# A window-attention gradient on one core: computing the gradient of x as (dS·x)·Aᵀ, with dS·x turned by DMA

## The chip, the cores and the metric

The kernel runs on one core of a Trainium2 chip. The metric is the device time of one execution in microseconds; lower is better.

Names used in the profile: PE is TensorE's matmul, PEld its weight load, ACT ScalarE, DVE VectorE, POOL GpSimd, SP SyncE. SPq and POOLq are the queues on which SyncE and GpSimd issue DMAs; the page calls their rings q1 and q0. L126 is line 126 of that run's kernel, so the same operation has other line numbers before and after.

## The reference

Attention in windows of 8x8 pixels on an image of 256x256 pixels with 384 channels, forward and backward:

```python
xw  = windows(x)                       # 1024 windows, 64 tokens, C = 384
q, k, v = split(xw @ wqkv)
p   = softmax(q k^T * C**-0.5)
out = unwindow((p v) @ wo)
# returned: out, and the gradients of x, wqkv, wo for a given grad_out
```

All in bfloat16. The kernel folds the weights once: A = scale·Wq·Wkᵀ, so that the scores are x·A·xᵀ, and B = Wv·Wo, so that the output is P·(x·B). With dS the gradient of the scores, the gradient of x is the sum of three terms: a term of dS with x·Aᵀ (called v in the kernel before), the term of dSᵀ with x·A, and the term of Pᵀ with grad_out·Bᵀ. The last two are called y and z; they are made with channels on the partitions and have to be turned to tokens-on-partitions (`tok`) by a DMA.

## The kernel before

Work goes in quads of four tiles of 128 tokens (two windows each); 128 quads in all. In one step quad c is finished, quad b is in the middle and quad a begins. Everything that SyncE issues goes through one queue, in order:

```python
def load(st):                               # x on SyncE's queue, grad_out on GpSimd's
    ...
    for t in range(QUAD):
        nc.sync.dma_start(out=xq[:, t, :], in_=dram_tile(x, bp, t0 + t))
        nc.gpsimd.dma_start(out=dq[:, t, :], in_=dram_tile(grad_out, bp, t0 + t))

def load_turn(st):                          # dT and xT: both turned by DMA
    ...
            nc.sync.dma_start_transpose(out=dst[:, k:]..., in_=src[:, k:]...)

def to_tokens(st):                          # tok: y and z turned by DMA
    nc.sync.dma_start_transpose(out=tok[:]..., in_=st["yz"][:]...)

def uv(st, t, part):                        # u = x B (part 0) and v = x A^T (part 1)
    wgt, dst, cp = ((B_sb, st["uq"], ...), (AT_sb, st["vq"], ...))[part]
    pj = ring.tile([P, C], F32, tag="r")    # ring: 8 PSUM banks for everything
    for m in range(CK):
        product(pj[:], st["xT"][:, t, m, :], wgt[:, m, :], m == 0, m == CK - 1)
    cp(out=dst[:, t, :], in_=pj[:])

def attend(st, pair, after=None):
    for t in pair:                          # two tiles: 2 x 4 = 8 banks
        po, pu, pw, pd = [ring.tile([P, C], F32, tag="r", name=n) for n in ("po", "pu", "pw", "pd")]
        both((pu, "ST", "xq", True), (po, "PT", "uq", True))     # 64x64 products, four at once
        ...                                 # evictions of po (ACT) and pu (DVE)
        both((pw, "Pb", "dq", True), (pd, "ST", "vq", False))    # pd: the v term of dx
        ...
    for t, pd in made:                      # the y and z terms on top, from tok
        for w, o in ((0, HI), (1, LO)):
            nc.tensor.matmul(pd[o, :], lhsT=st["ps"][:, w, t, :], rhs=st["tok"][:, :, t, w, :], start=False, stop=True)
        ...                                 # eviction (ACT) and store of dx
```

`filler(1)` puts one piece of the weight gradients (24 products, then an addition into `GF_acc` by VectorE, which frees that piece's PSUM bank) before each of the two calls of `attend`.

Of the kernel before, what the change touches and what calls it, by code (L numbers as in the profile page):

```python
# [14 lines left out]
P = 128  # L15
# [7 lines left out]
def kernel(  # L23
# [12 lines left out]









# [7 lines left out]
    scale = float(C) ** -0.5  # L52

    const = ctx.enter_context(tc.tile_pool(name="const", bufs=1))
    setup = ctx.enter_context(tc.tile_pool(name="setup", bufs=1))
    grp = ctx.enter_context(tc.tile_pool(name="grp", bufs=2 * GQ + 1))
    qp = ctx.enter_context(tc.tile_pool(name="qp", bufs=2))
    sm = ctx.enter_context(tc.tile_pool(name="sm", bufs=2))
# [8 lines left out]
    wo_sb = const.tile([P, CK, C], BF16)  # L67
    nc.scalar.dma_start(out=wo_sb[:], in_=wo.rearrange("(m p) n -> p m n", p=P))

    wT_sb = setup.tile([P, JK, C], BF16, tag="big")  # L70
    for jm in range(JK):
        pt = ring.tile([P, C], BF16, tag="r")
        for m in range(CK):
            nc.tensor.transpose(pt[:, m * P:(m + 1) * P], w_sb[:, m, jm * P:(jm + 1) * P], ident[:])
        nc.vector.tensor_copy(out=wT_sb[:, jm, :], in_=pt[:])
# [11 lines left out]
    for dst, left, lo, right, ro, sc in (  # L87
        (A_sb, wT_sb, 0, wT_sb, CK, scale),
        (BT_sb, wo_sb, 0, wT_sb, 2 * CK, None),
        (B_sb, wT_sb, 2 * CK, wo_sb, 0, None),  # L90
        (AT_sb, wT_sb, CK, wT_sb, 0, scale),
    ):
        for mr in range(CK):
            pc = ring.tile([P, C], F32, tag="r")
            for mc in range(CK):
                nc.tensor.matmul(pc[:], lhsT=left[:, lo + mc, mr * P:(mr + 1) * P], rhs=right[:, ro + mc, :],
                                 start=(mc == 0), stop=(mc == CK - 1))
            if sc is None:
                nc.vector.tensor_copy(out=dst[:, mr, :], in_=pc[:])
            else:  # L100
                nc.scalar.activation(out=dst[:, mr, :], in_=pc[:], func=ACT.Copy, scale=sc)
# [8 lines left out]
    OTHER = {0: HI, WT: LO}  # L110
# [9 lines left out]
    def load_turn(st):  # L120
        xq, dq = st["xq"], st["dq"]
        st["xT"] = xT = qp.tile([P, QUAD, CK, P], BF16, tag="xT", name="xT", bufs=3)
        st["dT"] = dT = qp.tile([P, QUAD, CK, P], BF16, tag="dT", name="dT")
        for src, dst in ((dq, dT), (xq, xT)):
            k = G_ON_PE if src is dq else 0
            if k < QUAD:  # L126
                nc.sync.dma_start_transpose(out=dst[:, k:].rearrange("p t m k -> p (t m) k"),
                                            in_=src[:, k:].rearrange("p t c -> p (t c)"))

    def grad_turn(st, t):  # L130
        if t >= G_ON_PE:
            return
        pt = ring.tile([P, CK, P], BF16, tag="r")
        for m in range(CK):
            nc.tensor.transpose(pt[:, m, :], st["dq"][:, t, m * P:(m + 1) * P], ident[:])
        nc.vector.tensor_copy(out=st["dT"][:, t, :, :], in_=pt[:])

    ALL = False
    split = [ALL]

# [7 lines left out]
    ENG = {"D": nc.vector.tensor_copy, "A": nc.scalar.copy}  # L148

    def project(st, kind, mo):  # L150
        if kind == 0 and mo == 0:
            st["yz"] = qp.tile([P, CK, QUAD, 4, WT], BF16, tag="yz", name="yz")
        yz = st["yz"]
        wgt, src = ((BT_sb, st["dT"]), (A_sb, st["xT"]))[kind]
        pj = ring.tile([P, QUAD, 2, WT], F32, tag="r")
# [3 lines left out]
        if kind == 0:  # L159
            ENG[EV["z"][mo]](out=yz[:, mo, :, 0:4:3, :], in_=pj[:])  # L160
        else:
            ENG[EV["y"][mo]](out=yz[:, mo, :, 1:3, :], in_=pj[:])  # L162

# [5 lines left out]
    def scores(st):  # L169
        yz, xT = st["yz"], st["xT"]  # L170
        st["sd"] = sd = ring.tile([P, QUAD, 2, WT], F32, tag="r", name="sd")
        for t in range(QUAD):
            for w in range(2):
                for m in range(CK):
                    product(sd[:, t, w, :], yz[:, m, t, 2 * w:2 * w + 2, :].rearrange("p s k -> p (s k)"),
                            xT[:, t, m, w * WT:(w + 1) * WT], m == 0, m == CK - 1)
# [4 lines left out]
    def soft(st, step):  # L181
# [14 lines left out]
        elif step == 3:  # L196
            ex = st["ex"]
            rs = sm.tile([P, QUAD], F32, tag="rs")
            nc.vector.tensor_reduce(out=rs[:], in_=ex[:], axis=AX.X, op=ALU.add)
            ri = sm.tile([P, QUAD], F32, tag="ri")  # L200
# [3 lines left out]
            st["ps"] = ps = qp.tile([P, 2, QUAD, WT], BF16, tag="ps", name="ps")  # L204
            for w, h in ((0, LO), (1, HI)):
                nc.scalar.copy(out=ps[h, w, :, :], in_=Pb[h, :, :])  # L206
# [6 lines left out]
        else:  # L213
            pd = sm.tile([P, QUAD, WT], F32, tag="pd")
# [4 lines left out]

    def uv(st, t, part):  # L220
        if t == 0 and part == 0:
            for n in ("uq", "vq"):
                st[n] = qp.tile([P, QUAD, C], BF16, tag=n, name=n)
        wgt, dst, cp = ((B_sb, st["uq"], ENG[EV["u"][t]]), (AT_sb, st["vq"], ENG[EV["v"][t]]))[part]
        pj = ring.tile([P, C], F32, tag="r")
        for m in range(CK):
            product(pj[:], st["xT"][:, t, m, :], wgt[:, m, :], m == 0, m == CK - 1)
        cp(out=dst[:, t, :], in_=pj[:])  # L228

    def turn(st):  # L230
        pt = ring.tile([P, QUAD, 2, WT], F32, tag="r", name="pt")
        for t in range(QUAD):
            for w, h in ((0, LO), (1, HI)):
                nc.tensor.matmul(pt[h, t, :, :].rearrange("p s k -> p (s k)"), lhsT=st["ps"][:, w, t, :],  # L234
                                 rhs=ident[:], start=True, stop=True)
        st["PS"] = dst = qp.tile([P, QUAD, 2, WT], BF16, tag="PS", name="PS")
        nc.vector.tensor_copy(out=dst[:], in_=pt[:])

    def turned(st, n, t, h):
        if n in ("PT", "ST"):  # L240
            return st["PS"][h, t, int((n == "ST") == (h == LO)), :]
        return st[n][h, t, :]

    def store(dst, src, bp, t):
        for h, w in ((LO, 1), (HI, 0)):
            nc.gpsimd.dma_start(out=dram_tile(dst, bp, t)[WIN * w:WIN * (w + 1)], in_=src[h, :])  # L246

    def attend(st, pair, after=None):
        bp, t0 = st["at"]
        if pair[0] == 0:  # L250
            st["Uq"] = grp.tile([P, QUAD, C], BF16, tag="Uq", name="Uq")
            st["Wq"] = grp.tile([P, QUAD, C], BF16, tag="Wq", name="Wq")
        def both(straight, crossed):
            for h, o, (dst, lhs, rhs, done) in ((LO, LO, straight), (LO, HI, crossed), (HI, LO, crossed),
                                                (HI, HI, straight)):
                nc.tensor.matmul(dst[o, :], lhsT=turned(st, lhs, t, h), rhs=st[rhs][h, t, :], start=True, stop=done)  # L256

        made = []
        for t in pair:
            po, pu, pw, pd = [ring.tile([P, C], F32, tag="r", name=n) for n in ("po", "pu", "pw", "pd")]  # L260
            both((pu, "ST", "xq", True), (po, "PT", "uq", True))
            osb = ob.tile([P, C], BF16, tag="o")
            ENG[EV["o"][t]](out=osb[:], in_=po[:])  # L263
            ENG[EV["U"][t]](out=st["Uq"][:, t, :], in_=pu[:])  # L264
            both((pw, "Pb", "dq", True), (pd, "ST", "vq", False))
            ENG[EV["W"][t]](out=st["Wq"][:, t, :], in_=pw[:])  # L266
            made.append((t, pd))
            store(out_0, osb, bp, t0 + t)
        for t, pd in made:
            for w, o in ((0, HI), (1, LO)):  # L270
                nc.tensor.matmul(pd[o, :], lhsT=st["ps"][:, w, t, :], rhs=st["tok"][:, :, t, w, :], start=False,  # L271
                                 stop=True)
            dsb = ob.tile([P, C], BF16, tag="d")
            ENG[EV["d"][t]](out=dsb[:], in_=pd[:])  # L274
            store(out_1, dsb, bp, t0 + t)
        if after is not None:
            turn(after)
# [3 lines left out]
    def gf_group(sts):  # L281
        n = len(sts) * QUAD
        for f in range(2):
            for ma in range(CK):
                pw = ring.tile([P, C], F32, tag="r", name="pg")
                for i in range(n):
                    st, t = sts[i // QUAD], i % QUAD
                    product(pw[:], st["xq"][:, t, ma * P:(ma + 1) * P], st["UW"[f] + "q"][:, t, :], i == 0, i == n - 1)
# [11 lines left out]
    def step(c, b, a):  # L300


        def on(st):
            return (lambda f, *r: f(st, *r)) if st is not None else (lambda f, *r: None)
        C_, B, A = on(c), on(b), on(a)
        B(scores)
        B(soft, 0)
        B(uv, 0, 0)
        B(uv, 0, 1)
        B(soft, 1)  # L310
        B(uv, 1, 0)
        B(uv, 1, 1)
        B(soft, 2)
        B(soft, 3)
        B(uv, 2, 0)
        B(uv, 2, 1)
        for t in range(QUAD):
            A(grad_turn, t)
        B(uv, 3, 0)
        B(uv, 3, 1)  # L320
        B(soft, 4)
        for mo in range(CK):
            A(project, 0, mo)
        B(soft, 5)
        filler(1)
        if c is not None:
            attend(c, (2, 3), b)
        else:
            B(turn)
        split[0] = True  # L330
        for mo in range(CK):
            A(project, 1, mo)
        A(to_tokens)
        filler(1)
        split[0] = ALL
        B(attend, (0, 1))

    G_ON_PE = 0
    EV = {"z": "AAA", "y": "AAA", "u": "AAAA", "v": "AAAA", "o": "AAAA", "U": "DDDD", "W": "DDDD", "d": "AAAA"}
    quads = [(bp, t0) for bp in range(NBP) for t0 in range(0, NT, QUAD)]  # L340
    sts = [{"at": q, "i": i} for i, q in enumerate(quads)]
    n = len(sts)
    AHEAD = 3
    with tc.manual_schedule(engines=MANUAL):
        for i in range(min(AHEAD, n)):
            load(sts[i])
            if i < AHEAD - 1:
                load_turn(sts[i])
        held = []
        get = lambda i: sts[i] if 0 <= i < n else None  # L350
        for i in range(-1, n + 1):
            if AHEAD <= i + AHEAD < n:
                load(sts[i + AHEAD])
# [71 lines left out]
```

## Time and profile before

| | before |
|---|---|
| time, median | 2045.04 us of 3 runs (2043.45 to 2060.44) |
| PE, ACT, DVE, POOL busy | 99, 72, 67, 69% |
| SyncE's queue q1, GpSimd's queue q0 | 75.0%, 31.7% of 16 engines' span |
| one step (pu to pu) | 15.62 us |

From the page of the kernel before: the busy time of each engine, the row of DMA busy tenths in 40 slices, the two queues (packets, MB, share of 16 engines' span), and the shares of the chain that ended last.

```profile
PE 2025.2 (99%) x20442; PEld 1148.8 (56%) x20442; DVE 1382.3 (67%) x3107; ACT 1467.0 (72%) x3213; POOL 1419.1 (69%) x2566
...
DMA  9999999999999999999999999999999999999992
...
q1 hardware_dynamic: 873648, 253.80, 75.0%
q0 software_dynamic: 122880, 151.68, 31.7%
...
PE 91%; DMA 2%; ACT 1%; DVE 1%; issue 0%; POOL 0%; ACTq 0%; POOLq 0%
```

PE is busy for nearly the whole span and makes up 91% of the chain, so the kernel is bound by PE. The shares of the two queues add up to 106.7%.

Now the timeline of PE over one pair of `attend` (start in us, length in us, engine, line, operation, number of instructions merged):

```profile
1005.26 0.35 PE L256 MATMUL pu<-xq,PS 64*64 64x384 bf16 x1
...
1005.45 0.33 PE L256 MATMUL pd<-vq,PS 64*64 64x384 bf16 x2
...
1005.77 0.32 PE L256 MATMUL pw<-dq,Pb 64*64 64x384 bf16 x1
1005.99 0.35 PE L256 MATMUL pd<-vq,PS 64*64 64x384 bf16 x2
...
1006.27 0.52 PE L271 MATMUL pd<-tok,ps 128*64 128x384 bf16 x4
...
1020.88 0.35 PE L256 MATMUL pu<-xq,PS 64*64 64x384 bf16 x1
```

and VectorE's line of the same moment:

```profile
1005.38 0.56 DVE L289 TENSOR_TENSOR GF_acc<-pg,GF_acc 128x384 f32<-128x384 f32 x1 [2.56 <-PE pg L144]
```

The second pd should start together with the pw at 1005.77, as the first pd did with its own pw. It starts at 1005.99, 50 ns after the addition into `GF_acc` ended (1005.38 + 0.56 = 1005.94). The pair wants eight banks, and the eighth is still held by the weight-gradient piece. From the first pu to tok it takes 1.01 us; from this first pu to that of the next step (1020.88) 15.62 us.

The timeline of SyncE's queue over a step (the length is that of the issue, not of the transfer):

```profile
1004.03 4.98 SPq L166 DMA_TRANSPOSE tok<-yz  x1
1009.06 2.58 SPq L117 DMA_DIRECT2D xq<-in_x_dram  x4
1011.81 1.74 SPq L127 DMA_TRANSPOSE dT<-dq  x1
1013.60 2.56 SPq L127 DMA_TRANSPOSE xT<-xq  x1
1019.65 4.28 SPq L166 DMA_TRANSPOSE tok<-yz  x1
```

After xT (to 1016.16) the queue issues nothing until 1019.65: 3.5 us here.

### The profile page before, as it was taken

Reading aid. Unit: us, or ns where it says so; the run is one execution under the profiler, and the core shown is the slowest. Engines: PE = TensorE matmul, PEld = TensorE weight load, DVE = VectorE, ACT = ScalarE, POOL = GpSimd, SP = SyncE. Lnnn points to the kernel's source line nnn. Section 1 sums busy time; section 2 is a strip of 40 time slices with the busy share of each in tenths; the row PEclk is TensorE's granted clock in tenths of the full one; section 3 lists DMA queues with packets and bytes.
Section 4 is the critical chain, followed back from the end, with each engine's and each line's share of the span. In section 5 each row is a group of like instructions: output and inputs, shape, how many; then the busy total and the mean of one; then the engine's idle time right before and its main releaser. Section 6 shows DMA issues by size and latency. Waiting matters only on the chain.

```text
span 2049.9 us, 54462 instructions
## 1 busy us (share of the span) xinstructions
PE 2025.2 (99%) x20442; PEld 1148.8 (56%) x20442; DVE 1382.3 (67%) x3107; ACT 1467.0 (72%) x3213; POOL 1419.1 (69%) x2566
## 2 busy tenths in 40 slices
PE   7999999999999999999999999999999999999998
PEld 4555555555555555555555555555555555555555
DVE  5766666666667666666666666666666666666665
ACT  5866677777777777777777777777777777777773
POOL 4766767676767767777677767777677777667764
PEclk9999999999999999999999999999999999999999
DMA  9999999999999999999999999999999999999992
GB/s 204 220 190 195 193 198 219 200 203 204 201 207 204 204 200 205 211 203 205 202 205 202 204 199 203 208 203 208 199 204 206 201 200 209 198 200 202 212 179 78
DMA packets 997192, 409.25 MB, mean 200 GB/s; under 512 B 880704, under 2 KB 971584, under 8 KB 996928
## 3 DMA queue, kind: packets, MB, share of 16 engines
q1 hardware_dynamic: 873648, 253.80, 75.0%
q0 software_dynamic: 122880, 151.68, 31.7%
q8 instruction: 159, 2.61, 0.6%
q14 instruction: 105, 0.86, 0.1%
q10 hardware_dynamic: 400, 0.29, 0.0%
HBM read 101.84 MB, written 101.84 MB: 99 GB/s over the span
## 4 chain that ended last, share of the span: by engine, by line
PE 91%; DMA 2%; ACT 1%; DVE 1%; issue 0%; POOL 0%; ACTq 0%; POOLq 0%
PE pj L146 33%; PE pg L146 12%; PE pg L144 11%; PE pj L144 11%; PE pd L271 5%; PE pu L256 5%; PE sd L146 5%; PE pw L256 4%; PE pd L256 3%; PE pt L234 1%; DMA out_dram<-dsb 1%; DMA out_dram<-osb 1%; ACT uq L228 0%; ACT vq L228 0%; DMA dq<-in_grad_out_dram 0%
## 5 line engine op out<-in xcount | busy, mean ns | idle before, releaser
L246 POOL DMA_DIRECT2D out_dram<-osb x1024 | 576.8, 570 | 339.9 <-ACT osb L263 179.3
L246 POOL DMA_DIRECT2D out_dram<-dsb x1024 | 571.3, 563 | 218.3 <-DMA dq<-in_grad_out_dram 68.3
L289 DVE TENSOR_TENSOR GF_acc<-pg,GF_acc 128x384 f32<-128x384 f32 x258 | 143.8, 557 | 460.3 <-PE pg L144 319.6
L146 PEld LDWEIGHTS <-xT 128*128 128x128 bf16 x3072 | 291.7, 98 | 186.2 <-issue 4.5
L263 ACT CAST osb<-po 128x384 bf16<-128x384 f32 x512 | 221.7, 484 | 231.9 <-PE pu L256 174.6
L146 PE MATMUL pj<-AT_sb,xT 128*128 128x384 bf16 x1536 | 333.9, 327 | 2.1 <-ACT dsb L274 1.9
L146 PE MATMUL pj<-B_sb,xT 128*128 128x384 bf16 x1536 | 334.3, 327 | 0.0
L118 POOL DMA_DIRECT2D dq<-in_grad_out_dram x512 | 274.0, 550 | 51.6 <-issue 14.5
L228 ACT CAST uq<-pj 128x384 bf16<-128x384 f32 x512 | 247.6, 484 | 71.3 <-PE pj L146 67.1
L264 DVE CAST Uq<-pu 128x384 bf16<-128x384 f32 x512 | 280.3, 548 | 7.0 <-PE pu L256 6.9
L266 DVE CAST Wq<-pw 128x384 bf16<-128x384 f32 x512 | 280.2, 547 | 0.0
L146 PE MATMUL pj<-dT,BT_sb 128*128 128x512 bf16 x1152 | 269.6, 379 | 1.0 <-ACT ps L206 1.0
L144 PE MATMUL pj<-xT,A_sb 128*64 128x512 bf16 x2304 | 270.1, 379 | 0.0
L274 ACT CAST dsb<-pd 128x384 bf16<-128x384 f32 x512 | 222.2, 483 | 56.6 <-DMA out_dram<-dsb 18.6
L228 ACT CAST vq<-pj 128x384 bf16<-128x384 f32 x512 | 250.4, 489 | 2.8 <-PE pj L146 0.5
L162 ACT CAST yz<-pj 128x512 bf16<-128x512 f32 x384 | 223.9, 587 | 30.8 <-PE pj L144 0.4
L256 PE MATMUL pw<-dq,Pb 64*64 64x384 bf16 x1024 | 226.9, 329 | 1.3
L144 PEld LDWEIGHTS <-xq 128*64 128x64 bf16 x3000 | 171.5, 110 | 86.1 <-issue 1.0
L146 PEld LDWEIGHTS <-xq 128*128 128x128 bf16 x1572 | 153.0, 98 | 117.4 <-DVE pr L210 3.2
L256 PEld LDWEIGHTS <-PS 64*64 64x64 bf16 x3072 | 120.3, 105 | 165.5 <-issue 152.5
L206 ACT COPY ps<-Pb 64x256 bf16<-64x256 bf16 x256 | 103.2, 403 | 149.6 <-DVE Pb L203 148.1
L160 ACT CAST yz<-pj 128x512 bf16<-128x512 f32 x384 | 206.4, 645 | 0.3 <-PE pj L146 0.2
(64 smaller groups left out, 2723.4 us busy)
## 6 DMA issues: line engine op xcount, KB each, us to landing
xq<-in_x_dram SPq DMA_DIRECT2D x512, 96.0 KB, 4.1
dq<-in_grad_out_dram POOLq DMA_DIRECT2D x512, 96.0 KB, 5.2
out_dram<-osb POOLq DMA_DIRECT2D x1024, 48.0 KB, 4.7
out_dram<-dsb POOLq DMA_DIRECT2D x1024, 48.0 KB, 4.5
dT<-dq SPq DMA_TRANSPOSE x128, 5.9
xT<-xq SPq DMA_TRANSPOSE x128, 7.5
tok<-yz SPq DMA_TRANSPOSE x128, 8.7
w_sb<-in_wqkv_dram SPq DMA_DIRECT2D x1, 864.0 KB, 5.5
```

Of the source, the lines that this page charges most:

```text
L118: nc.gpsimd.dma_start(out=dq[:, t, :], in_=dram_tile(grad_out, bp, t0 + t))
L144: nc.tensor.matmul(out[h], lhsT=lhsT[:, h], rhs=rhs, start=start, stop=stop)
L146: nc.tensor.matmul(out, lhsT=lhsT, rhs=rhs, start=start, stop=stop)
L160: ENG[EV["z"][mo]](out=yz[:, mo, :, 0:4:3, :], in_=pj[:])
L162: ENG[EV["y"][mo]](out=yz[:, mo, :, 1:3, :], in_=pj[:])
L228: cp(out=dst[:, t, :], in_=pj[:])
L246: nc.gpsimd.dma_start(out=dram_tile(dst, bp, t)[WIN * w:WIN * (w + 1)], in_=src[h, :])
L256: nc.tensor.matmul(dst[o, :], lhsT=turned(st, lhs, t, h), rhs=st[rhs][h, t, :], start=True, stop=done)
L263: ENG[EV["o"][t]](out=osb[:], in_=po[:])
L264: ENG[EV["U"][t]](out=st["Uq"][:, t, :], in_=pu[:])
L266: ENG[EV["W"][t]](out=st["Wq"][:, t, :], in_=pw[:])
L274: ENG[EV["d"][t]](out=dsb[:], in_=pd[:])
```

## The change

Intent: instead of v = x·Aᵀ for every token and then dS·v, make U = dS·x, which the weight gradient needs anyway (`Uq`), and multiply it by Aᵀ. The 12 v products per quad are replaced by 12 U·Aᵀ products, but the 64x64 products dS·v go altogether. U has tokens on its partitions and the product needs channels there, so U is turned by one more DMA transpose per quad (`UT`). To give UT and tok time to land, a quad's gradient `dx` is made two steps after its scores; tok is issued at the start of the next step, and the buffers are shuffled to make room (`yz` gets 3, the soft-max tiles 1). dx is stored in one DMA per tile instead of two halves. The core of the diff:

```diff
-def uv(st, t, part):                      # u and v
+def values(st, t):                        # u alone
 ...
+def to_channels(st, src, name):
+    st[name] = dst = qp.tile([P, QUAD, CK, P], BF16, tag=name, name=name, bufs=3 if name == "xT" else 2)
+    nc.sync.dma_start_transpose(out=dst[:]..., in_=st[src][:]...)
 ...
-            st["yz"] = qp.tile([P, CK, QUAD, 4, WT], BF16, tag="yz", name="yz")
+            st["yz"] = qp.tile([P, CK, QUAD, 4, WT], BF16, tag="yz", name="yz", bufs=3)
 ...  # attend: per pair 2 x (po, pu) + 2 pw = 6 banks, three groups instead of four
+        for t in pair:
+            po, pu = [...]
+            both((pu, "ST", "xq", t), (po, "PT", "uq", t))
+            ...
+        pw = [ring.tile([P, C], F32, tag="r", name="pw") for t in pair]
+        both((pw[0], "P", "dq", pair[0]), (pw[1], "P", "dq", pair[1]))
 ...
+    def dx(st, pair):                     # two steps on
+        for t, pd in zip(pair, pds):
+            for w, o in ((0, LO), (1, HI)):
+                nc.tensor.matmul(pd[o, :], lhsT=st["ps"][:, w, t, :], rhs=st["tok"][:, :, t, w, :], ...)
+        for t, pd in zip(pair, pds):
+            for m in range(CK):
+                product(pd[:], st["UT"][:, t, m, :], AT_sb[:, m, :], False, m == CK - 1)
+            ...                           # eviction, one store of 128 partitions
 ...  # the step
+        pw = C_(attend, (2, 3))
+        pt = B(turn)
+        ...
+        C_(to_channels, "Uq", "UT")
+        C_(attend_end, (2, 3), pw)        # half of the Wq evictions moves to ACT
+        D_(dx, (0, 1))
+        filler(1)
+        pw = B(attend, (0, 1))
+        B(attend_end, (0, 1), pw)
+        D_(dx, (2, 3))
```

(The diff also moves the set-up tiles to other pools. Per step SyncE's queue now takes: dT, xT, four loads, tok, UT.)

## The prediction

> **What bounds the kernel now.** TensorE. The page gives PE 99% busy at full clock (PEclk 9), ACT 72%, DVE 67%, POOL 69%; the chain that ended last is 91% PE. In the timeline one quad's step repeats every 15.62 us (pu at 1005.26 to 1020.88), and 128 steps make about 2000 of the 2045 us. The chain in order of time splits a step: z 1.94, y 1.94, u and v together 3.9, two gradient pieces 2 x 1.95, scores 0.81, turn 0.22, and two "attend" pairs of 1.01 (the 64x64 products) plus 0.45 (tok).
>
> **What goes, comes, moves.**
> 1. PE: 12 v products of 128x384 per quad go, 12 UT*A^T products come, each 0.16 us start to start: nothing gained.
> 2. The dS*v 64x64 products go: per pair four groups of four concurrent products become three, one group start-to-start 0.16 us.
> 3. A second gain in the same place. A pair now takes po, pu, pw, pd twice: all 8 PSUM banks. The eighth (second pd) waits for the GF_acc addition: GF_acc ended at 1005.94, 1015.98 and 1021.55; the blocked pd started at 1005.99, 1016.03 and 1021.60 each time. The profile calls the neighbouring weight loads' waits "issue" (about 152 us in the waits view), so this is hidden in "busy". First pu to first tok is 1.00 us; without the stall I estimate 0.79, and with three groups on six banks 0.63. Leaving a tiling mode still costs a drain (the Trainium skill, "TensorEngine Tiling (Array Packing)", Key Properties, says a mode switch drains): last group to tok 0.28 against 0.16 between groups. The number of switches stays.
>    Saved: 0.37 x 2 per step = 0.74, so PE's step falls to 14.88 and PE's total by about 95 us.
> 4. ACT: 4 v evictions (0.49) go, 4 half-Wq copies (estimate 0.45) come: even. DVE loses 2 Wq copies (0.55): to about 9.7 us of a step. POOL issues 16 DMAs instead of 20 per quad. None bounds.
> 5. DMA: one more transpose per quad (UT), 0.39 MB on top of 1.57 MB of transposes. The transfers view has SP's queue at 75% of 16 engines and POOL's at 32%; UT adds about 2.5 us per step (estimate: transposes' share of it, scaled by bytes). On the SP queue a step issues loads 2.5 to 3.3, dT 1.9, xT 2.8, tok 4.3 to 5.5 us: about 12.7. With UT 14.5 to 15.5, all but PE's new 14.88. UT and tok have a step of slack, so latency is hidden; throughput of the SP queue is not. I expect it to give back part: a step of about 15.1.
>
> **Critical path.** All of 2 and 3 lie on it. 5 becomes a second bound nearly equal to PE. Fill and drain of the deeper pipeline: within 3 us either way.
>
> **Predicted: 1975 us**, 8 in 10 between 1945 and 2018. Faster by over 2%: 0.73; within 2%: 0.21; slower: 0.06.
>
> **What would show it.** pu to the next turn or tok about 0.63 us, and no stall behind GF_acc; PE step 14.9 where it has no wait; PE wait on "UT" or "tok" DMAs if SP bounds; SP issuing with hardly a gap, its queue share near 90% or more; GB/s about 230 instead of 200; Wq half copies about 0.45 us.
>
> **What would make it wrong.** Transposes that slow down under the added traffic, so that the SP queue's cycle goes past 15.6 us (no gain or a loss); or a queue that drains faster than I think (1950 or a little below); a new PSUM-bank wait, above all dx's pd tiles waiting for ACT's po evictions; PE waiting for soft-max in the shorter stretch between scores and turn.

## The result

| | before | after |
|---|---|---|
| time, median | 2046.31 us (4 runs, 2043.45 to 2060.44) | 2150.9 us (4 runs, 2137.53 to 2154.13) |
| ratio, 95% interval | | 1.0489 [1.0432, 1.0545]: slower |
| span and granted clock of the profiled run | 2049.9 us, 0.999 | 2135.8 us, 0.986 |
| PE, ACT, DVE, POOL busy | 99, 72, 67, 69% | 95, 68, 60, 53% |

The median of before is that of the runs made in the same rounds as those of after. All ratios here are the mean time of one kernel's fast runs over the mean of the other's fast runs of the same rounds, so they are not quite the ratio of the medians quoted. The prediction of 1975 us was wrong, and in direction: a loss of 5% where a gain of 3% was expected.

From the page of after, the lines that answer to those of before, and ScalarE's costliest idle group (busy, mean ns | idle before, releaser). The page's chain that ended last breaks off after 1% in this run and is of no use.

```profile
PE 2021.4 (95%) x19046; PEld 1183.3 (55%) x19046; DVE 1280.2 (60%) x2851; ACT 1455.3 (68%) x3213; POOL 1122.7 (53%) x2054
...
DMA  9999999999999999999999999999999999999995
...
q1 hardware_dynamic: 1074384, 304.15, 85.6%
q0 software_dynamic: 98304, 151.39, 27.5%
...
L138 ACT CAST yz<-pj 128x512 bf16<-128x512 f32 x384 | 213.4, 588 | 360.6 <-DMA tok<-yz 328.0
```

PE's busy time has hardly fallen (2025.2 to 2021.4 us), although 1396 fewer matmuls are issued; e1 below issues just as many as after and is busy for 1922.1 us. So some 100 us of what the page counts as busy in after is lost time, on top of the 5% that it shows as idle. It is stalling for the most part; the lower granted clock (0.986, in e1 1.000) can make up 30 us of it at most (an estimate: 1.4% of the span). ScalarE, which never bounded before, now stands for 328 us in front of one copy, the eviction of z into `yz`, waiting for the DMA that turns an older `yz`. The waits view of after (us in total, times, longest) has that wait in second place (behind one of GpSimd for ScalarE, 637.3), and further down the waits of PE that follow from it:

```profile
ACT yz L138 <- DMA tok<-yz: 328.0, 99, 7.2
...
PEld L242 <- issue: 226.6, 525, 4.2
...
PE po L242 <- ACT yz L138: 45.5, 72, 3.9
```

The timeline of SyncE's queue after:

```profile
1002.01 6.15 SPq L144 DMA_TRANSPOSE tok<-yz  x1
1008.25 1.47 SPq L116 DMA_TRANSPOSE UT<-Uq  x1
1009.94 3.12 SPq L116 DMA_TRANSPOSE dT<-dq  x1
1013.24 1.69 SPq L116 DMA_TRANSPOSE xT<-xq  x1
1014.98 2.89 SPq L111 DMA_DIRECT2D xq<-in_x_dram  x4
1017.98 6.78 SPq L144 DMA_TRANSPOSE tok<-yz  x1
1024.85 2.88 SPq L116 DMA_TRANSPOSE UT<-Uq  x1
...
1032.22 3.38 SPq L111 DMA_DIRECT2D xq<-in_x_dram  x4
```

From 1002.01 to 1024.85 each issue starts within 0.25 us of the end of the one before: the gap of before is gone, SyncE does not stand waiting for Uq before it issues UT, and one cycle (tok to tok) takes 15.97 us here; the neighbouring cycle, from loads at 1014.98 to loads at 1032.22, takes 17.24. This is longer than the 15.62 us of before's whole step. The queue sets the pace. How it reaches PE is seen ten microseconds on, first on ScalarE:

```profile
1029.05 1.07 ACT L138 CAST yz<-pj 128x512 bf16<-128x512 f32 x2 [3.85 <-DMA tok<-yz]
```

then on PE:

```profile
1030.18 0.45 PE L242 MATMUL pu<-xq,PS 64*64 64x384 bf16 x2
1031.49 0.35 PE L242 MATMUL po<-uq,PS 64*64 64x384 bf16 x2 [0.85 <-ACT yz L138]
```

tok was issued at 1017.98 and had not read its `yz` buffer until 1029; of three such buffers none was free; ScalarE stood idle before the z eviction for 3.85 us; the PSUM banks whose evictions come after it in the program were not emptied; and PE, which had run on into the free banks, stopped at 1030.64 for the next bank. A late DMA thus slows PE by way of an engine that is 68% busy: PE does not wait for the DMA, nor for the buffer that the DMA still reads, but for a PSUM bank.

In numbers over a longer stretch: I took every issue of SyncE's queue between 600 and 1100 us from the timeline (29 to 34 steps) and averaged. "Step" is the sum divided by the share of the time in which the queue was issuing. Over the whole run the sums differ from these by 0.2 us at most (after: 15.6).

| mean issue, us | dT | xT | 4 loads | tok | UT or extra | sum | share issuing | step |
|---|---|---|---|---|---|---|---|---|
| before | 1.95 | 2.85 | 2.91 | 4.88 | | 12.59 | 0.81 | 15.6 |
| after | 2.94 | 2.18 | 2.76 | 5.35 | 2.48 | 15.71 | 0.96 | 16.4 |
| e1_no_ut | 1.79 | 2.85 | 3.19 | 5.02 | | 12.85 | 0.87 | 14.8 |
| e4_before_extra | 3.01 | 2.89 | 2.59 | 5.71 | 2.45 | 16.65 | 0.97 | 17.2 |
| e13_x_one_issue | 2.94 | 2.43 | 0.84 | 6.22 | 2.58 | 15.01 | 0.96 | 15.6 |

The last three rows are experiments, told next. The waits view also names releasers for these issues (mostly the latest ScalarE eviction, on which most of them do not depend), so I don't read causes from it there; the experiments decide.

One thing the records do show: the length of an issue is not a fixed cost. dT, xT and UT are transposes of the same shape, and UT's issue alone took between 1.42 and 3.95 us in after. In e6 below, where U is copied and not turned, UT's issue falls from 2.48 to 0.64 us (same window), but xT's grows from 2.18 to 3.49 and tok's from 5.35 to 5.69. So a part of an issue's length is time in which it is held up, and what one issue saves comes back in part in the others.

### The profile page after: what moved, and what is told of

The parts are those of the page before. It is cut to its first block, busy times and chain, and to the rows that moved or that the text cites. A ratio compares the mean times of both kernels' runs of the same rounds, so it can differ in the third digit from the quotient of the medians.

```text
span 2135.8 us, 51378 instructions
## 1 busy us (share of the span) xinstructions
PE 2021.4 (95%) x19046; PEld 1183.3 (55%) x19046; DVE 1280.2 (60%) x2851; ACT 1455.3 (68%) x3213; POOL 1122.7 (53%) x2054
## 3 DMA queue, kind: packets, MB, share of 16 engines
q1 hardware_dynamic: 1074384, 304.15, 85.6%
## 5 line engine op out<-in xcount | busy, mean ns | idle before, releaser
L231 POOL DMA_DIRECT2D out_dram<-osb x1024 | 578.3, 571 | 682.9 <-ACT osb L249 637.3
L233 POOL DMA_DIRECT2D out_dram<-dsb x512 | 275.4, 541 | 136.4 <-DMA out_dram<-dsb 62.4
L126 PE MATMUL pv<-B_sb,xT 128*128 128x384 bf16 x1536 | 270.6, 326 | 0.0
L126 PE MATMUL pj<-xT,A_sb 128*128 128x512 bf16 x1152 | 269.5, 379 | 0.9 <-DMA xT<-xq 0.9
L224 ACT CAST uq<-pv 128x384 bf16<-128x384 f32 x512 | 242.7, 475 | 35.5 <-PE pv L126 33.3
L261 ACT CAST Wq<-pw 64x384 bf16<-64x384 f32 x512 | 242.5, 474 | 9.2
L126 PEld LDWEIGHTS <-A_sb 128*128 128x128 bf16 x1152 | 112.6, 98 | 137.1 <-DMA xT<-xq 1.4
L242 PE MATMUL po<-uq,PS 64*64 64x384 bf16 x1024 | 145.0, 338 | 45.9 <-ACT yz L138 45.5
L126 PEld LDWEIGHTS <-xT 128*128 128x128 bf16 x1536 | 141.5, 98 | 82.8
L124 PE MATMUL pg<-Wq,xq 128*64 128x384 bf16 x2016 | 182.0, 329 | 0.0
L126 PE MATMUL pg<-Uq,xq 128*128 128x384 bf16 x1032 | 181.6, 326 | 0.0
## 6 DMA issues: line engine op xcount, KB each, us to landing
tok<-yz SPq DMA_TRANSPOSE x128, 10.2
```

Source lines behind the costliest of these rows:

```text
L124: nc.tensor.matmul(out[h], lhsT=lhsT[:, h], rhs=rhs, start=start, stop=stop)
L126: nc.tensor.matmul(out, lhsT=lhsT, rhs=rhs, start=start, stop=stop)
L224: nc.scalar.copy(out=st["uq"][:, t, :], in_=pj[:])
L231: nc.gpsimd.dma_start(out=to[WIN * w:WIN * (w + 1)], in_=src[h, :])
L233: nc.gpsimd.dma_start(out=to, in_=src[:])
L261: nc.scalar.copy(out=st["Wq"][h, pair[1], :], in_=pw[1][o, :])
```

## The experiments

Theory: SyncE's queue is the bound of after, through the work that stands in it. Rivals: the latency of tok (then one more buffer helps); the bytes of all queues together on the shared DMA engines (then it doesn't matter from which queue bytes are taken); and an error on PE's side of the sum (then the change doesn't pay without UT's transpose either). e6 and e7 are wrong by design, but pass the comparison, presumably because the term they spoil is small.

### e1_no_ut: PE's side alone

UT is not turned; the products read a tile filled once (dx wrong).

```diff
-                product(pd[:], st["UT"][:, t, m, :], AT_sb[:, m, :], False, m == CK - 1)
+                product(pd[:], UT_any[:, t, m, :], AT_sb[:, m, :], False, m == CK - 1)
-        C_(to_channels, "Uq", "UT")
```

> The changed kernel without the transpose of dS*x (UT<-Uq): the products with A^T read one tile that is filled once, by one transpose of x at the start (gradient of x wrong on purpose). Theory 1 (the SP queue with one transpose more can't pass a quad in less than 16.5 us; its delay reaches TensorE over tok, yz and ScalarE): the queue's cycle falls to about 13.5 us, TensorE's own 15.13 us a step binds, time about 1985 us (1960 to 2010). Rival A (the new order on TensorE, ScalarE and PSUM is slower in itself): stays above 2090. Rival B (too few yz buffers, not throughput): some gain, but tok is as slow as before, above 2040.

Measured: 1945.5 us (1944.0 to 1948.3), ratio 0.9482 [0.9453, 0.9511], below the range I gave, which rested on too long a step for PE (15.13 us). The timeline of PE over a pair in e1:

```profile
1014.07 0.35 PE L242 MATMUL pu<-xq,PS 64*64 64x384 bf16 x1
...
1018.27 0.35 PE L242 MATMUL pu<-xq,PS 64*64 64x384 bf16 x1
...
1018.47 0.33 PE L242 MATMUL po<-uq,PS 64*64 64x384 bf16 x2
...
1018.62 0.33 PE L242 MATMUL pw<-dq,Pb 64*64 64x384 bf16 x4
1018.89 0.52 PE L267 MATMUL pd<-tok,ps 128*64 128x384 bf16 x4
...
1028.90 0.35 PE L242 MATMUL pu<-xq,PS 64*64 64x384 bf16 x1
```

First pu to tok is 0.62 us against 1.01 before, and the step is 14.83 us (from 1014.07 to 1028.90). The whole difference between e1 and after, 205 us, is one transpose per quad. The rival about PE's side falls: its part of the change works as computed.

### e4_before_extra: the transpose alone, in the kernel before

The kernel before, with one transpose of `Uq` per quad added, into a tile that nobody reads (correct).

```diff
+        if c is not None:
+            extra = setup.tile([P, QUAD, CK, P], BF16, tag="big", name="extra")
+            nc.sync.dma_start_transpose(out=extra[:]..., in_=c["Uq"][:]...)
```

> The kernel before with one more transpose per quad, Uq into a tile that nobody reads, at the place where the change has it; results right. Theory 1: the SP queue's cycle grows from about 13 us to 15.5 to 16.5 us, at or over TensorE's 15.62, so 2050 to 2150 us and the SP queue without gaps. Rival A: 2045, within 1% of the kernel before.

Measured: 2199.33 us, ratio 1.0711 [1.0676, 1.0745]: some 150 us for a transfer whose result nothing reads, and above the range I gave. SyncE's queue in e4:

```profile
999.45 6.54 SPq L166 DMA_TRANSPOSE tok<-yz  x1
1006.08 2.50 SPq L117 DMA_DIRECT2D xq<-in_x_dram  x4
1008.76 3.09 SPq L127 DMA_TRANSPOSE dT<-dq  x1
1011.90 3.06 SPq L127 DMA_TRANSPOSE xT<-xq  x1
1015.05 1.48 SPq L332 DMA_TRANSPOSE extra<-Uq  x1
1016.62 6.95 SPq L166 DMA_TRANSPOSE tok<-yz  x1
```

The same picture as after, in the old kernel: no gap, and the other issues have grown with it (tok 4.98 and 4.28 before, 6.54 and 6.95 here; dT 1.74, here 3.09). The extra issue is the shortest of all; its price shows in its neighbours. The gap of 3 us before was not 3 us of room. So the loss needs neither the new schedule nor the later gradient.

### e3_yz4: one more buffer

```diff
-            ... name="yz", bufs=3)
+            ... name="yz", bufs=4)
```

> The changed kernel with four yz buffers instead of three, so that ScalarE may run one quad further ahead of the tok transpose. Theory 1 (throughput of the SP queue): a buffer more only moves the wait to another place, time within 1% of the changed kernel (2125 to 2160). Rival B (a latency that one more buffer hides): 1980 to 2060.

Measured: 2146.62 us, ratio 1.0472 [1.0438, 1.0506], as after. The waits view of e3:

```profile
PEld L124 <- DMA UT<-Uq: 133.7, 108, 4.2
...
PE pd L124 <- DMA UT<-Uq: 97.4, 102, 3.8
...
PE pd L267 <- DMA tok<-yz: 43.6, 47, 3.4
```

ScalarE no longer waits for tok at all, and PE now waits for UT and tok itself. The path by way of ScalarE is how the bound shows, not the bound. The latency of tok falls as a rival; that of UT, which got no further buffer here, falls with e11 below, where UT is turned as in after and PE is 99% busy.

### e6_ut_copy and e7_ut_half: bytes or turning, and how much of it

e6 copies U without turning it (same bytes); e7 turns half of it and uses it twice.

```diff
-        C_(to_channels, "Uq", "UT")
+            nc.sync.dma_start(out=c["UT"][:]..., in_=c["Uq"][:]...)                          # e6
+            nc.sync.dma_start_transpose(out=c["UT"][:]..., in_=c["Uq"][:, 0:2, :]...)        # e7
```

> The changed kernel with UT made by a plain copy of the same 0.39 MB on the same queue at the same place, not turned (gradient of x wrong on purpose). If it is the turning in 256-byte packets that costs: TensorE binds at 14.83 us a step, 1940 to 1970. If it is the bytes: near the changed kernel, over 2080. If it is one more long DMA to wait for on SP, whatever it moves: over 2000.

> The changed kernel with only half of UT turned (two tiles of four, used twice; gradient of x wrong on purpose). Theory 1 as a throughput limit: the cycle of the DMA side falls by half of what a whole UT costs, from 16.5 to about 14.9, so nearly TensorE's 14.83: 1950 to 2000. If what costs is the fact of one more transpose between the others (not its size): over 2060.

Measured: e6 2023.43 us (ratio 0.9906 [0.9873, 0.9940]), which is the third case that I had named, one more long DMA to wait for; e7 2012.31 us (ratio 0.9843 [0.9816, 0.9870]), between my two ranges. Over e1 (0.9482), the plain copy costs 4.2% of the time before, half a transpose 3.6%, the whole one 10.1%. Turning costs more than copying, but copying isn't free, and the cost is not proportional: half the transpose costs 3.6 and the other half 6.5. I read this as PE still binding for a part of the first half. In e6 the engines moved 228 GB/s on the page, in after 215, so 215 is no ceiling of bytes.

### e5_fewer_stores and e12_no_dq_loads: fewer bytes on the other queue

e5 stores the output for one tile of four; e12 loads grad_out only once (both wrong). Both take traffic from GpSimd's queue alone.

```diff
-            store(out_0, st, t, osb, True)
+            if t == 0:
+                store(out_0, st, t, osb, True)          # e5
-            nc.gpsimd.dma_start(out=dq[:, t, :], in_=dram_tile(grad_out, bp, t0 + t))   # e12
```

> The changed kernel, but the output o is stored for one tile of each quad only (output 0 wrong on purpose): 0.29 MB less per quad on GpSimd's queue, nothing changed on SP's queue. If the 16 DMA engines as a whole are the limit: GpSimd's transfers took 27.5% of the engines' time, a quarter of which goes, so about 1 us of 16.5 a step, 1990 to 2060. If SP's own issue or ring is the limit: no change, 2120 to 2160.

> The changed kernel without the loads of grad_out in the loop (four quads loaded once, used over and over; all outputs wrong on purpose). The twin of the run without loads of x: the same 0.39 MB of the same shape from HBM, but on GpSimd's queue. If the 16 engines as a whole are the limit, it gains as that run did: 1944 to 1990. If what counts is the work that stands in SP's own queue: little, 2080 to 2140.

Measured: e5 2122.78 us, ratio 1.0393 [1.0340, 1.0447], about 1% less than after for 0.29 MB less per quad, but its interval overlaps that of after (1.0432 to 1.0545). e12 2067.14 us, ratio 1.0110 [1.0084, 1.0136], about 4% less for 0.39 MB less per quad, between my two ranges. The other queue's traffic does count, but in part.

### e11_no_x_loads and e13_x_one_issue: less in SyncE's own queue

e11 loads x only once (wrong): the same 0.39 MB per quad as e12, but from SyncE's queue. e13 loads as many bytes in rows of the same length, from a wrong place, with one transfer instead of four (wrong).

```diff
-            nc.sync.dma_start(out=xq[:, t, :], in_=dram_tile(x, bp, t0 + t))            # e11 and e13
+        nc.sync.dma_start(out=xq[:], in_=...[q:q + 512, :].rearrange("(t p) e -> p t e", p=P))   # e13
```

> The changed kernel without the loads of x in the loop: four quads of x are loaded once and used over and over (all outputs wrong on purpose), every transpose stays. It measures what the loads cost the DMA side. If the transposes alone are the limit (1.97 MB at their own rate): 2080 to 2150. If the loads' 2.9 us of SP issue count in full: 16.5 less 2.9, so TensorE binds, 1945 to 1970. If only their bytes count (0.39 of 3.54 MB, 11%): about 14.9, 1950 to 2000. The runs with x on other queues, which were slower, speak for the first.

> The changed kernel with x loaded by one transfer per quad instead of four, the same bytes in the same 768-byte rows on SP's queue, from rows in another order (outputs wrong on purpose). If SP's issue of four short loads (2.9 us) is what the loads cost: 1950 to 2010. If it is the moving of their bytes among the transposes: 2100 to 2150. The run with the loads spread between the transposes (2091) lets expect something between.

Measured: e11 1944.2 us, ratio 0.9486 [0.9466, 0.9505]; PE is 99% busy and the time that of e1. From e11's page:

```profile
PE 1922.8 (99%) x19046; PEld 1104.3 (57%) x19046; DVE 1264.6 (65%) x2851; ACT 1462.9 (75%) x3213; POOL 1122.9 (58%) x2054
```

e13 2048.25 us, ratio 1.0007 [0.9981, 1.0033]. So 0.39 MB off SyncE's queue is worth at least 10% (then PE binds), and off GpSimd's 4%. Issuing the loads as one saves about 5% with the same bytes: up to half of what the loads cost is that there are four of them. (e13 also reads x in another order from HBM; no run separates that.) Its issue takes 0.84 us in place of 2.76 (the table above); tok grows from 5.35 to 6.22 and eats a part of it. The Trainium skill ("DMA: Bandwidth & Descriptors", Issuing engines are not separate DMA queues) says that the sequencer's time for initiating a DMA "is usually small relative to the DMA itself". For one load that is so here (0.7 us of issue, a median of 3.7 us from issue to landing in after), for tok less so (5.35 of 10.2 us); but all issues of a step follow one another in one queue and add up to 15.7 of its 16.4 us.

### e2_x_on_pool and e9_x_on_act: the loads on another queue

```diff
-            nc.sync.dma_start(out=xq[:, t, :], ...)
+            nc.gpsimd.dma_start(out=xq[:, t, :], ...)      # e2
+            nc.scalar.dma_start(out=xq[:, t, :], ...)      # e9
```

> The changed kernel with the four loads of x per quad issued by GpSimd instead of SP; every byte still moves. If the limit is SP's queue (its issue and its rings): SP loses about 2.8 us of 16.5 a step, TensorE binds at about 15.1, time 1970 to 2010. If the limit is the 16 DMA engines as a whole: the same bytes, time within 2% of the changed kernel, 2110 to 2160. Rival A: unchanged too.

> The changed kernel with the four loads of x per quad issued by ScalarE on its own hardware queue: SP's queue is relieved of 2.8 us of issue, GpSimd's is not lengthened as in the run with x on GpSimd, the bytes stay. If SP's issue or ring is the limit: 1960 to 2050. If the 16 engines as a whole are: 2100 to 2170. ScalarE pays some 2 us of issue per step, which still fits in a step.

Measured: e2 2416.9 us, ratio 1.1743; e9 2229.93 us, ratio 1.0886; both correct, both far slower than after, which neither theory had. In e2 GpSimd's own groups show another wait: the profile puts its idle time before a store down to loads that come in (in after, for the osb stores, 637.3 us of 682.9 to ScalarE's eviction).

```profile
L231 POOL DMA_DIRECT2D out_dram<-osb x1024 | 580.7, 572 | 490.1 <-DMA dq<-in_grad_out_dram 184.7 <-DMA xq<-in_x_dram 99.2 <-ACT osb L249 45.6
...
L233 POOL DMA_DIRECT2D out_dram<-dsb x512 | 275.6, 541 | 362.4 <-DMA xq<-in_x_dram 141.7 <-DMA dq<-in_grad_out_dram 113.0 <-ACT uq L224 42.0
```

In e9 ScalarE's own work comes later: VectorE waits 337.5 us for its exponentials, 81.0 us in after. Both runs put the loads into a queue that has duties of its own, so they say nothing clean about SyncE's queue; whether a really idle queue would help stays open. The skill's rule that spreading DMAs over the engines does not help for bandwidth ("DMA: Bandwidth & Descriptors", Rules for kernel authors) agrees in direction; here it even cost 4% and 12% over after.

### e10_x_between: another order

The four loads stand between the transposes instead of in one block (correct): load, UT, dT, load, xT, two loads, tok.

> The changed kernel with the four loads of x spread between the transposes on SP's queue instead of one after the other; same bytes, same queue, results right. If the queue runs dry while SP issues four short loads in a row[...]: 2000 to 2070 us. If the queue's transposes are limited by their own rate all the time: 2120 to 2160.

Measured: 2090.61 us, ratio 1.0222 [1.0179, 1.0265], 2.5% less than after with the same transfers, and between my two ranges. The order alone is worth that much; why was not tested.

### e8_ut_pe2 and e14_pe2_between: a version that takes work off the queue

e8 turns U of two of the four tiles on PE against the identity, with a copy by VectorE, and leaves two to the DMA (correct). e14 is e8 with the order of e10 (correct).

```diff
+    def turn_u(st, t):
+        pt = ring.tile([P, CK, P], BF16, tag="r", name="pU")
+        for m in range(CK):
+            nc.tensor.transpose(pt[:, m, :], st["Uq"][:, t, m * P:(m + 1) * P], ident[:])
+        nc.vector.tensor_copy(out=st["UT"][:, t, :, :], in_=pt[:])
 ...
+        for t in range(2):
+            D_(turn_u, t)
-        C_(to_channels, "Uq", "UT")
+            nc.sync.dma_start_transpose(out=c["UT"][:, 2:]..., in_=c["Uq"][:, 2:, :]...)
```

> The changed kernel with UT of two tiles of a quad turned by TensorE and copied by VectorE, and of the other two by DMA (results right; a candidate to beat both). The run with half of UT turned by DMA had 2008 us; TensorE pays six more turns of about 0.1 us per step (14.83 to about 15.5). Theory 1: both sides nearly equal at about 15.4, so 2000 to 2045 us. If the DMA side did not matter: 2030 or more from TensorE alone.

> Half of UT turned by TensorE, and the loads of x spread between the transposes; results right, the candidate for a version better than both. Six turns cost TensorE 0.34 us in the run with half of UT on TensorE, so its own step is 15.17 us; the DMA side falls below that (16.5 less 1.15 less 0.4). 1990 to 2008 us, faster than the kernel before by 2 to 3%.

Measured: e8 2011.07 us, ratio 0.9832 [0.9776, 0.9888]; e14 2005.08 us (2002.68 to 2010.49), ratio 0.9804 [0.9779, 0.9828]. PE's timeline in e14:

```profile
1011.43 0.50 PE L283 MATMUL pU<-ident,Uq 128*128 128x128 bf16 x6
1011.77 2.11 PE L130 MATMUL pg<-Uq,xq 128*128 128x384 bf16 x12
```

Six turns hold PE up for 0.34 us (1011.43 to the start of the next product, 57 ns each), far less than the queue's price; VectorE pays two copies of 0.35 us per step. e14 beats both kernels (by about 2% over before; its interval is wholly below 1, but does not settle whether it is over 2%). About 3.2% (0.9804 against 0.9482) still lie between it and e1, which has no UT transpose at all.

Two further builds never reached the chip: an extra transpose into a tile of its own found no room, and a correct load of four tiles in one DMA needed an access pattern of more than three dimensions.

## Why the prediction was wrong

**PE bounds the kernel before, and items 1 to 3 (right).** The trade of v for U·Aᵀ is neutral, and the fourth group of 64x64 products and the stall on the PSUM bank are worth what was computed: step 14.83 us measured in e1, 14.88 predicted; pair 0.62 us measured, 0.63 predicted; about 105 us in all, predicted 95. e1 agrees with the drain that the skill puts at a change of tiling mode ("TensorEngine Tiling (Array Packing)", Key Properties): 0.27 us from the last pw group to tok, against 0.15 between the last two groups (1018.47 to 1018.62). How the saving splits between the fourth group and the stall was read from the trace only; no run separates them.

**ACT, DVE and POOL don't bound (right as far as it went).** The half-Wq copies took 474 ns, estimated 450. But ScalarE does carry the queue's lateness on to PE. That path was not foreseen: I named only PE waiting for UT or tok, which is what e3 shows once the fourth buffer is there.

**Latency of UT and tok is hidden (right).** e3 for tok, e11 for UT.

**Item 5, the step that failed: "With UT 14.5 to 15.5 ... I expect it to give back part: a step of about 15.1."** That SyncE's queue becomes a second bound was right, and so was the size of UT's own issue (2.5 us estimated, 2.48 measured). What failed is the size of the queue's cycle: 16.4 us. By the table of mean issues, of the 1.3 us too many some 0.5 are issues that grew when the queue filled (15.71 in sum, where 12.7 + 2.5 = 15.2 was counted; dT grew by 1.0 and tok by 0.5, xT shrank by 0.7), and 0.7 are the short spaces between issues, which remain in a queue that never pauses: it issues 96 to 97% of the time, and I had let it run at 100% (the rest, 0.1, is rounding). The times give the same step without the table: e1 takes 14.83, and after is 205 us / 128 = 1.60 longer, 16.43. 128 steps x 1.3 us are 166 us; the prediction with this one term replaced gives 1975 + 166 = 2141, and 2137.53 was the time of the profiled run. So the miss needs no second term. (This is bookkeeping with the measured cycle; that the queue makes the cycle is what e1, e4 and e11 show.)

**Why it was mis-sized.** Two readings of before's profile. The gap of about 3 us per step in SyncE's queue and the share of 75% were read as room, and durations taken from a queue with gaps were kept as constants. In all runs where the queue sets the pace (after, e3, e4, e5, e10, e12, e13) its share on the page stands at 84.6 to 87.9% and not near 100. (e11 and e14 reach 84.7 and 84.6% with PE 99% busy: the share alone doesn't tell a full queue from a nearly full one.) Scaled by the page, after's need could have been worked out only with that figure in hand: 85.6% of 16.4 us against 75% of 15.6 us is 14.0 against 11.7 of engine time per step, so UT's addition of 2.3 is near the estimate; how high the share can go is what was missing. e4 shows that it takes no restructuring.

**"What would make it wrong" named the outcome**, a cycle past 15.6 us, and put it down to transposes that slow down under the added traffic. Their issues did lengthen, in sum; the packets did not: by the pages (share x 16 engines x span / packets) a packet of SyncE's queue took 28.2 ns before and 27.2 ns after on average. A loss of over 2% was given 6% and should have been given far more, since the expected 15.1 left half a microsecond.

**Still open.** Why the queue's share stays below 88%, and whether that lies in the issuing of descriptors or in the turning itself: e13 (issues) and e6 (turning) each recover a part, and e2 and e9 are clouded by their own waits.

## What to carry to other kernels

Here a queue that issued transposes and paused 3 us per step did not have 3 us to give, and its issue times grew as it filled; before a restructuring that rests on one more DMA, add that DMA to the old kernel, unread, and time it. When a DMA sets the pace, look for it where it doesn't show its name: an engine standing at a copy whose buffer a late DMA still reads, and behind that PE waiting for PSUM. Moving a few transposes to the engine that bounds (57 ns each here) can be cheaper than giving them to the queue that is about to.

## What the Trainium skill lacked or had wrong

- "DMA: Bandwidth & Descriptors", Issuing engines are not separate DMA queues, calls the time to initiate a DMA usually small beside the DMA. That holds for one load here (0.7 of 3.7 us), but not for the sum in one queue: four loads of 96 KB take 2.76 us of issue per step of 16.4, all issues 15.7, and one issue of the same bytes in place of four took about 5% off the kernel (e13).
- The same page, Latency and other measured facts, has 261 GB/s for DMA transposes of one kernel (with a non-contiguous middle dimension). Here SyncE's queue, issuing transposes and loads without a pause, moved 304 MB in 2136 us, 142 GB/s, beside 71 GB/s on GpSimd's queue. No page says what a transposing queue reaches beside other traffic; its share stayed at 84.6 to 87.9% here where it set the pace.
- No page says that plain loads moved to GpSimd's or ScalarE's queue can slow the kernel: +12% (e2) and +4% (e9) over after, with GpSimd's idle time in e2 put down to earlier loads.
- "TensorE: Matmul & The Clock Gate", Part 4, puts a 128x128 turn on PE at about 390 ns alone and 275 ns in a kernel. One turn lasted 220 ns here, and six in a row held PE up for only 0.34 us, 57 ns each; that figure is the one that decides whether to turn on PE, and Part 4 lacks it (Part 1 has one for back-to-back matmuls, not for turns).
